# The order of copies, casts, sums and loads in one stage of a Fourier-mixing kernel

## The chip, the core and the metric

The kernel runs on one core of one Trainium2 chip. The metric is the device time of one execution in microseconds (us). TensorE is PE in the profile, its weight loads are PEld, VectorE is DVE, ScalarE is ACT, GpSimd is POOL, and SyncE (SP) issues most of the DMAs.

## What is computed

The input x has 2048 rows of 448 numbers. It is normalised, goes through a Fourier mixing and through a gated feed-forward network, and the two are multiplied:

```
xn = _layernorm(x, axis=-1)
# _A_ref
a = jnp.einsum("bsd,ed->bse", xn, dft_hid_re)
b = jnp.einsum("bsd,ed->bse", xn, dft_hid_im)
s = jnp.einsum("ts,bse->bte", dft_seq_re, a) - jnp.einsum("ts,bse->bte", dft_seq_im, b)
# _B_ref
g = _silu((_gelu(xn @ w_gate) * (xn @ w_up)) @ w_down)
return x + s * g
```

## The kernel before

The work has three parts, one behind the other: the feed-forward network (up to about 396 us of the span), the stage that computes a and b (396 to 484 us), and the sums along the sequence (from 484 us to the end). Numbers are kept in two parts, a high one that ACT casts from the full number and a low one that DVE gets as the difference, so a product takes two or three matmuls.

**The stage of a and b.** The 2048 rows are 16 tiles of 128. Tiles 0 to 7 are computed plainly: `hid_mm` issues 22 matmuls into two of the eight PSUM banks (a in one, b in the other). The other eight are computed as four pairs, tile 8+kk with tile 12+kk, by products of sums that save matmuls: `hid_pair` issues 39 matmuls into five banks, x1 (5 matmuls), x2 (6), x3 (5), x4 (5), then six more on top of x1, x6 (6), and six more on top of x4. Banks are given out in turn, so the one that was used eight tiles of PSUM ago must have been read.

After the matmuls a plain tile k goes through these steps: `hid_sums` has ACT copy the two banks into a scratch f in SBUF, `f_sums` has DVE make four differences within it (four instructions), `hid_split` has ACT cast the seven columns of f to the high part in the tile's place `TS[k]` (the 128x1568 ACTIVATE), and the function that it returns has DVE make the low part (the 128x1568 TENSOR_TENSOR). For tiles 0 to 3 the result is stored to DRAM (`td`), since its place is needed again. A pair has, between its products: ACT copies x1 to a scratch u (line 1298), DVE adds x2 to it (1301), makes c21 with x3 (1305) and a half of f with x4 (1288), ACT copies x1 again after its second round (1313), DVE makes another half with x6 (1288) and the last one with u and x4 (1321); then sums, casts and low parts for both tiles as above. The six matmuls on top of x1 can't start before ACT has copied x1 the first time; the six on top of x4 can't start before DVE has read x4 (the first use of line 1288).

Order of issue: tiles 0 and 1, pair 0, tile 2, pair 1, tile 3, pair 2, pair 3, then tiles 4 to 7. Within that, every engine does its instructions strictly in the order in which the program gives them. In the kernel before, the cast of tile 2 stands ahead of pair 1's first copy of x1 on ACT, and so for the other pairs. The low part of the plain tile (`between`) stands between the fourth sum and the second round of x1.

**Scratch.** Tiles 0 to 3, 8 to 11 and 4 use one f, in `raw`; tile 5 has one of its own (`f5`, tag g0); tiles 6, 7 and 12 to 15 share `f1` (tag d0), so tile 7's copies out of PSUM must wait for the low part of tile 6.

**Chunk 1.** Tiles 4 to 7 read chunk 1 of the transposed input. Its SBUF place holds, during the pairs, sums that the pairs use as weights (`tq`), so the chunk lies in DRAM (`sp`) and is loaded back in four parts by `load_1`, each after the last use of its place in pair 3: part 3 after the product x2, part 2 after x3, part 0 after x4, part 1 after x6. Each part is one DMA of 512 KB, for high and low together. `hid_mm(4, 1)` puts the matmuls on part 1 last and goes through parts 0, 2, 3 before.

**The sums along the sequence.** They go through units, one for each k and pair of output tiles. `load_c` loads a unit's two blocks on SP, `sum_c` has DVE make two sums, `prep_c` casts (ACT), makes the low part (DVE) and starts the next load into the freed place. `seven` issues a unit's 14 matmuls, in seven banks; the seventh product of unit 0 goes to the bank that held tile 7's a. In the kernel before, units 4, 5, 9 and 10 have their raw place in `cc`, units 0 to 3 and 6 to 8 in `raw`; from unit 11 on five places are used in turn. Unit 2's sums are made by POOL. Units 4 and 5 are loaded after tile 7's matmuls.

Of the kernel before, what the change touches and what calls it, by code (L numbers as in the profile page):

```python
# [48 lines left out]
LAST = 3  # L49

# [9 lines left out]
def fnet_geglu(ctx: ExitStack, tc: tile.TileContext, xw, ca, ct, cp, et, wss, wd, out):  # L60
# [495 lines left out]
    with tc.manual_schedule():  # L556
# [671 lines left out]
        def hid_mm(k, last=None):  # L1228
            c, kk = divmod(k, 4)
            sl = slice(kk * P, (kk + 1) * P)  # L1230
            ps = [in_turn("all", f"ab{k}_{r}") for r in range(2)]
            mm = [
                (r, (xtl if n == 2 else xth)[c][:, b, sl], e_at[b][r + 2 * (n == 1)], b == last)
                for r in range(2)
                for n in range(3)
                for b in range(3 if n == 1 else 4)
            ]
            mm = [v for v in mm if not v[3]] + [v for v in mm if v[3]]
            turn_ = [[i for i, v in enumerate(mm) if v[0] == r] for r in range(2)]
            for n, (r, a, b, _) in enumerate(mm):  # L1240
                nc.tensor.matmul(  # L1241
                    ps[r][:, :D], a, b, start=n == turn_[r][0], stop=n == turn_[r][-1],
                    skip_group_check=True,
                )
            return [p[:, :D] for p in ps]
# [9 lines left out]
        def hid_pair(kk, between, load):  # L1255
# [3 lines left out]
            fs[kc], fs[ke] = f_at(kc), f_at(ke)  # L1259
# [9 lines left out]
            t, q = ts[1], tq[1]  # L1269

            def run(ps, *jobs, first=True):
                mm = []
                for x_, e in jobs:
                    if isinstance(e, tuple):
                        mm += [(x_[i], e[j]) for i, j in ((0, 0), (0, 1), (1, 0))]
                    else:
                        mm += [(v, e) for v in x_]
                for n, (a, b) in enumerate(mm):
                    nc.tensor.matmul(  # L1279
                        ps, a[:, sl], b, start=first and n == 0, stop=n == len(mm) - 1,  # L1280
# [3 lines left out]
            def x_tile(i):  # L1284
                return in_turn("all", f"hx{i}_{kk}")[:, :D]

            def minus(to, a, ps):
                nc.vector.scalar_tensor_tensor(
                    to, two_sides(a), -1.0, two_sides(ps), op0=ALU.mult, op1=ALU.subtract
# [3 lines left out]
            fc, fe = fs[kc], fs[ke]  # L1293
            ea, eb = (two_sides(fe[:, :D]), two_sides(fe[:, D : 2 * D])) if plain_ else (halves(fe, 0), halves(fe, 1))
            u, c21 = temps
            x1 = x_tile(1)
            run(x1, (b11, a11), (k3, e_at[3][0]))
            nc.scalar.activation(u, x1, AF.Copy)
            x2 = x_tile(2)
            run(x2, (t[2], s2), (q[2], s2q))  # L1300
            nc.vector.tensor_add(u, u, x2)
            load(3)
            x3 = x_tile(3)
            run(x3, (t[3], s3), (q[3], s3q))
            nc.vector.tensor_add(c21, u, x3)
            load(2)
            x4 = x_tile(4)
            run(x4, (t[1], s1), (q[1], s1q))
            minus(eb, c21, x4)
            load(0)  # L1310
            between()
            run(x1, (b21, a12), (k2[0], k2a), first=False)
            nc.scalar.activation(halves(fc, 0), two_sides(x1), AF.Copy)
            x6 = x_tile(6)
            run(x6, (t[4], a22), (q[4], k2b))
            minus(halves(fc, 1), c21, x6)
            load(1)
            f_sums(kc)
            low_c = hid_split(kc)
            run(x4, (b22, s4), (k2[1], s4q), first=False)  # L1320
            nc.vector.tensor_add(ea, two_sides(u), two_sides(x4))
            if plain_:
                h, l = [rest(v) for v in ((new["tmp"], a_x[0]), (new["u1"], new["u0"]))[ke - 14]]
                nc.scalar.activation(h, fe[:, : 2 * D], AF.Copy)
                low_c()
                nc.vector.tensor_sub(l, fe[:, : 2 * D], h)
                ab[ke] = [(h[:, r * D : (r + 1) * D], l[:, r * D : (r + 1) * D]) for r in range(2)]
            else:
                f_sums(ke)
                low_e = hid_split(ke)  # L1330
                low_c()
                low_e()
# [46 lines left out]
        nxt = {0: 3, 1: 6, 2: 7, 3: 8, 9: None, 10: None}  # L1379
# [35 lines left out]

        def prep_c(m):

            if m >= len(units):
                return
            n = (4 if isinstance(units[m][1], str) else 7) * P  # L1420
            h, l = [v[:, :n] for v in slot_at(m)]
            split(h, l, raw_at(m)[:, :n])
            c_hl[m] = h, l
            n = nxt.get(m, m + 5)
            if n:
                load_c(n)


        def load_1(k):

            v, w = [u.rearrange("p (i k d) -> p i k d", i=2, k=4)[:, :, k] for u in (a_x[1].bitcast(F32), sp)]
            nc.sync.dma_start(v, w)
# [5 lines left out]
        ps = hid_mm(0)  # L1438
        late[0]()
        late[1]()  # L1440
        for _ in range(3):
            send()
        hid_sums(0, ps)()
        low_ = hid_split(0)
        for _ in range(3):
            send()
        low_()
        while dq:
            send()
        nc.sync.dma_start(gs[:, 8 * D :], gacc[2].tensor[:, : 8 * D])  # L1450
        hid_sums(1, hid_mm(1))()
        behind = hid_split(1)
        hid_pair(0, behind, lambda k: None)
        for k in (2, 3):
            hid_sums(k, hid_mm(k))()
            behind = hid_split(k)
            hid_pair(k - 1, behind, lambda k: None)
        hid_pair(3, lambda: None, load_1)
        load_c(0)
        load_t(0, a_x[0])  # L1460
        load_t(1, place("g1", 8 * D))
        hid_sums(4, hid_mm(4, 1))()
        behind = hid_split(4)
        ps = hid_mm(5)
        behind()
        load_c(1)
        load_c(2)
        hid_sums(5, ps)()
        behind = hid_split(5)
        sum_c(0)  # L1470
        prep_c(0)
        ps = hid_mm(6)
        behind()
        hid_sums(6, ps)()
        behind = hid_split(6)
        sum_c(1)
        sum_c(2, nc.gpsimd)
        behind()
        sum_c(3)
        ps = hid_mm(7)  # L1480
        cc = sb.tile([P, 4 * D], F32, name="cc", tag="d1")
        load_c(4)
        load_c(5)
        prep_c(1)
        sums7 = hid_sums(7, ps)
        prep_c(2)
# [95 lines left out]
        for m, (j, k) in enumerate(units):  # L1582
# [87 lines left out]
            else:  # L1670
                if m:
                    prep_c(m + 3)
                if m == 4:
                    sums7()
                if m == 6:
                    hid_split(7)()
                    load_c(14)
                    load_c(15)
# [72 lines left out]
```

## Time and profile before

| | |
|---|---|
| median of 3 runs | 779.63 us (777.25 to 779.84) |
| the profiled execution | 779.22 us, of which 777.4 us are the span of the trace |
| mean granted clock of TensorE | 0.996 |
| busy, share of the span | PE 98%, PEld 88%, DVE 84%, ACT 46%, POOL 16% |

The span is read from the first to the last instruction of the program; all times of the trace below are counted from its start. "Idle before" in a row, in square brackets, is the time for which the engine stood still just before it, and what ended that.

### The profile page before, as it was taken

Reading aid. Unit: us, or ns where it says so; the run is one execution under the profiler, and the core shown is the slowest. Engines: PE = TensorE matmul, PEld = TensorE weight load, DVE = VectorE, ACT = ScalarE, POOL = GpSimd, SP = SyncE. Lnnn points to the kernel's source line nnn. Section 1 sums busy time; section 2 is a strip of 40 time slices with the busy share of each in tenths; the row PEclk is TensorE's granted clock in tenths of the full one; section 3 lists DMA queues with packets and bytes.
Section 4 is the critical chain, followed back from the end, with each engine's and each line's share of the span. In section 5 each row is a group of like instructions: output and inputs, shape, how many; then the busy total and the mean of one; then the engine's idle time right before and its main releaser. Section 6 shows DMA issues by size and latency. Waiting matters only on the chain.

```text
span 777.4 us, 11575 instructions
## 1 busy us (share of the span) xinstructions
PE 761.6 (98%) x4033; PEld 685.3 (88%) x4033; DVE 655.9 (84%) x1119; ACT 354.6 (46%) x511; POOL 121.9 (16%) x162
## 2 busy tenths in 40 slices
PE   9999999999999999999999879899999999999997
PEld 8988888888888888888889769899999999999997
DVE  7987788989999889998876875979788797979796
ACT  6866443434444344353433434545444444544451
POOL 1001422324133232232200001000000000000000
PEclk9999999999999999999999999999999999999999
DMA  8077574949486867658715265779696969788794
GB/s 292 17 220 229 126 237 134 276 138 256 151 220 217 233 247 174 212 161 256 202 52 250 93 223 219 228 232 302 233 337 212 342 218 331 221 282 280 248 307 152
DMA packets 83579, 170.31 MB, mean 219 GB/s; under 512 B 8256, under 2 KB 63424, under 8 KB 81728
## 3 DMA queue, kind: packets, MB, share of 16 engines
q1 hardware_dynamic: 78192, 143.05, 53.3%
q0 software_dynamic: 5184, 26.41, 15.7%
q8 instruction: 31, 0.51, 0.3%
q14 instruction: 28, 0.23, 0.1%
q10 hardware_dynamic: 144, 0.11, 0.0%
HBM read 146.01 MB, written 52.63 MB: 256 GB/s over the span
## 4 chain that ended last, share of the span: by engine, by line
PE 78%; DVE 13%; DMA 4%; ACT 3%; issue 2%; SPq 0%; DVEq 0%; ACTq 0%
PE p L1520 19%; PE x L449 18%; PE po L423 14%; PE p L1523 9%; PE py L1546 4%; PE x L461 3%; PE gu L372 3%; PE ab L1241 2%; PE gu L605 2%; PE hx L1279 1%; DMA xt<-sp 1%; DMA raw<-sums 1%; PE pt L207 1%; PE warm L574 1%; DMA out<-cc 1%
## 5 line engine op out<-in xcount | busy, mean ns | idle before, releaser
L423 PE MATMUL po<-wd,hs 128*128 128x448 f32 x672 | 146.2, 366 | 0.0
L423 PEld LDWEIGHTS po<-wd,hs 128*128 128x128 f32 x672 | 125.7, 188 | 12.5 <-DVE gacc L436 0.3
L449 PE MATMUL x<-xt,w 128*128 128x512 f32 x432 | 112.2, 390 | 0.0
L449 PEld LDWEIGHTS x<-xt,w 128*128 128x128 f32 x432 | 80.9, 188 | 16.3 <-DVE tmp L503 0.4
L449 PE MATMUL x<-t,w 128*128 128x512 f32 x276 | 80.4, 391 | 0.4 <-DVE tmp L539 0.4
L150 ACT ACTIVATE w<-raw 128x896 fp32r<-128x896 f32 (+1 forms) x59 | 53.6, 910 | 55.6 <-PE p L1520 25.6
L436 DVE TENSOR_TENSOR gacc<-gacc,po 128x448 f32<-128x448 f32 x96 | 58.6, 614 | 5.5 <-PE po L423 5.2
L526 ACT ACTIVATE hs<-tmp 128x512 fp32r<-128x512 f32 x24 | 15.2, 633 | 104.1 <-DVE tmp L524 104.1
L449 PEld LDWEIGHTS x<-t,w 128*128 128x128 f32 x276 | 51.7, 188 | 10.7 <-DVE tmp L539 0.8
L1520 PE MATMUL p<-xt,xt 128*128 128x448 f32 x168 | 54.8, 376 | 2.4 <-ACT f L1346 2.4
L1520 PE MATMUL p<-ts_g,w 128*128 128x448 f32 x168 | 55.5, 380 | 0.0
L1572 POOL DMA_DIRECT2D cc<-xw x14 | 12.3, 881 | 257.5 <-DVE raw L1411 96.1
L321 POOL TENSOR_TENSOR raw<-raw 128x256 f32<-128x256 f32 x23 | 18.9, 823 | 214.5 <-DMA raw<-wss 143.4
L150 ACT ACTIVATE w<-f 128x896 fp32r<-128x896 f32 (+1 forms) x34 | 30.2, 888 | 38.1 <-PE p L1520 14.8
L151 DVE TENSOR_TENSOR w<-raw,w 128x896 fp32r<-128x896 f32 (+1 forms) x40 | 41.8, 1045 | 4.4 <-ACT w L150 4.1
L1523 PE MATMUL p<-ts_g,w 128*128 128x224 f32 x168 | 44.9, 267 | 0.0
L1523 PE MATMUL p<-xt,xt 128*128 128x224 f32 x168 | 44.6, 265 | 0.0
L1241 PE MATMUL ab<-w,xt 128*128 128x448 f32 x128 | 35.3, 379 | 2.5 <-DMA xt<-sp 2.5
L1520 PE MATMUL p<-xt,w 128*128 128x448 f32 x112 | 36.4, 374 | 0.0
L1520 PEld LDWEIGHTS p<-xt,xt 128*128 128x128 f32 x168 | 31.6, 188 | 5.1 <-ACT f L1346 2.7
L1520 PE MATMUL p<-hs,w 128*128 128x448 f32 x112 | 36.0, 374 | 0.0
L1520 PEld LDWEIGHTS p<-ts_g,w 128*128 128x128 f32 x168 | 32.2, 192 | 2.5
(302 smaller groups left out, 1860.8 us busy)
## 6 DMA issues: line engine op xcount, KB each, us to landing
sums<-ca SPq DMA_DIRECT2D x16, 896.0 KB, 8.6
sums<-ca POOLq DMA_DIRECT2D x16, 896.0 KB, 9.3
raw<-ct SPq DMA_DIRECT2D x69, 192.0 KB, 4.3
raw<-wss SPq DMA_DIRECT2D x24, 512.0 KB, 3.7
xt<-td SPq DMA_DIRECT2D x24, 448.0 KB, 5.5
ts_g<-td SPq DMA_DIRECT2D x24, 448.0 KB, 6.3
raw<-sums SPq DMA_DIRECT2D x69, 128.0 KB, 4.2
f<-ct SPq DMA_DIRECT2D x39, 192.0 KB, 4.7
```

The source lines that it names most:

```text
L150: nc.scalar.activation(h, src, AF.Copy)
L151: nc.vector.tensor_sub(l, src, h)
L321: eng.tensor_add(r[:, 1:16:14], r[:, 0:14:13], r[:, 9:17:7])
L372: nc.tensor.matmul(ps[:, cols], a, xt[:, k, cols], start=n == 0, stop=n == len(mm) - 1)
L423: nc.tensor.matmul(po[:, :D], hs[:, a, kk * P : (kk + 1) * P], wdn[:, b, i], start=n == 0, stop=n == 5,)
L436: nc.vector.tensor_add(ga, ga, po[:, :D])
L449: nc.tensor.matmul(ps, a[i], b[j], start=first and n == 0, stop=n == 2, skip_group_check=True)
L461: nc.tensor.matmul(ps, a[0], x_, start=False, stop=True, skip_group_check=True)
L1241: nc.tensor.matmul(ps[r][:, :D], a, b, start=n == turn_[r][0], stop=n == turn_[r][-1], skip_group_check=True,)
L1520: nc.tensor.matmul(ps[q][:, :D], h, v, start=u % UN == 0, stop=False, skip_group_check=True)
L1523: nc.tensor.matmul(ps[q][:, :HD], l, v[:, :HD], start=False, stop=u % UN == NS - 1, skip_group_check=True,)
L1546: nc.tensor.matmul(p[:, e], w, v[:, e], start=n == 0, stop=n == 11)
```

## The change

All of it lies in the stage of a and b and the first units; the arithmetic is the same, and no matmul is added or left out. The calls that were written out one by one (`hid_pair`, `hid_mm`, `load_1` and so on) become small steps with names, and a list, `HID`, gives their order. In that order:

1. In each pair ACT copies x1 for the first time ahead of the cast of the plain tile before it.
2. The tail of a pair is mixed with the next one's start. For pairs 2 and 3, ACT casts for tile 14 and tile 10 after pair 3's first copy of x1, and DVE makes the low part of tile 14 between pair 3's c21 and its read of x4, and that of tile 10 behind that read. Tile 0's low part stands behind the last sums of the feed-forward network.
3. Chunk 1 is loaded in eight DMAs of 256 KB, high and low apart, at the same four points. Tile 4's matmuls go through parts 3, 2, 0, 1, tile 7's through 2, 0, 1, 3.
4. Scratch: tiles 4 and 5 get a double one (`f45`, tag g0), tile 7 gets `cc`, and units 4, 5, 9 and 10 get the places in `f1` (tag d0), so that every unit but the first follows one rule of five places in turn.
5. Units 1 and 2 are loaded ahead of the large loads of k = 0 and 1 (`td`), unit 2's sums go from POOL to DVE, and the casts of units 0 to 2 come earlier: unit 1's and 2's wait for tile 7's matmuls on parts 2 and 0.

Two lines of the list, and the core of the rest:

```diff
+HID = """
...
+P1.x1 P1.m 2.ca P1.x2 P1.u P1.x3 P1.c21 P1.x4 P1.be 2.lo P1.x1b P1.ac P1.x6 P1.bc P1.sc P1.cc
...
+7.mm c.h1 c.d1 c.h2 c.d2 6.ca c.s3 6.lo c.l4 c.l5 7.ev
+"""
 
         def f_at(k):
-            if k == 5:
-                return sb.tile([P, 8 * HD], F32, name="f5", tag="g0")
-            if k in (6, 7, 12, 13, 14, 15):
+            if k in (4, 5):
+                if "f" not in new:
+                    new["f"] = sb.tile([P, 16 * HD], F32, name="f45", tag="g0")
+                return new["f"][:, 8 * HD * (k - 4) :][:, : 8 * HD]
+            if k == 7:
+                return cc
+            if k in (6, 12, 13, 14, 15):
...
+            if order:
+                mm.sort(key=lambda v: order.index(v[1]))
...
         def raw_at(m):
-            if m in (4, 5, 9, 10):
-                return cc[:, 896 * ((m + 1) % 5) :][:, :896]
-            i = (2, 0, 1, 2, 0, 0, 0, 1, 2)[m] if m < 9 else (m - 11) % 5
+            i = (m + 4) % 5 if m else 2
             return a_r[:, 896 * i :][:, :896] if i < 3 else new["d0"][:, 896 * (i - 3) :][:, :896]
...
         def load_1(k):
 
-            v, w = [u.rearrange("p (i k d) -> p i k d", i=2, k=4)[:, :, k] for u in (a_x[1].bitcast(F32), sp)]
-            nc.sync.dma_start(v, w)
+            for i in range(2):
+                v, w = [u[:, 2048 * i + 512 * k :][:, :512] for u in (a_x[1].bitcast(F32), sp)]
+                nc.sync.dma_start(v, w)
...
+        orders = {4: (3, 2, 0, 1), 7: (2, 0, 1, 3)}
...
+        for word in HID.split():
+            a, b = word.split(".")
+            if word == "7.ev":
+                cc = sb.tile([P, 4 * D], F32, name="cc", tag="d1")
+            steps_[a][b]()
```

In the list, `mm` is a plain tile's matmuls, `ev` its copies out of PSUM, `sm` its sums, `ca` its cast, `lo` its low part; of a pair, `x1` to `x6` are products (`x1b` and `x4b` the second rounds), `m` the first copy of x1, `u`, `c21`, `be`, `ac`, `bc`, `ae` the steps named above in that order, `sc`, `cc`, `lc` sums, cast and low part of the tile 8+kk and `se`, `ce`, `le` those of 12+kk; `x.0` to `x.3` are the loads of chunk 1, `t.0` and `t.1` the large loads, `c.l`, `c.s`, `c.h`, `c.d` a unit's load, sums, cast and low part.

On ACT, from tile 2 (`ab2`) to pair 1 (`hx1_1` is x1 of pair 1), before:

```order
L1346 ACTIVATE raw_76<-ab2_0_3604 128x2x224
L1347 ACTIVATE raw_76<-ab2_1_3605 128x2x224
L1358 ACTIVATE hs0_77<-raw_76 128x7x224
L1298 ACTIVATE raw_76<-hx1_1_3635 128x448
L1313 ACTIVATE raw_76<-hx1_1_3635 128x2x224
```

The same place on ACT in the changed kernel:

```order
L1374 ACTIVATE raw_76<-ab2_0_3600 128x2x224
L1375 ACTIVATE raw_76<-ab2_1_3601 128x2x224
L1341 ACTIVATE raw_76<-hx1_1_3634 128x448
L1386 ACTIVATE hs0_77<-raw_76 128x7x224
L1349 ACTIVATE raw_76<-hx1_1_3634 128x2x224
```

The first copy of x1 has moved ahead of the cast of tile 2 (into `hs0`), which itself waits for DVE's sums of tile 2.

On SP, from the loads of chunk 1 (`xt1` from `sp`) through the large loads (from `td0`, `td1`), before:

```order
L1432 DMA xt1_68<-sp_810 128x2x512 x4
L1404 DMA raw_76<-ct 128x384
L1405 DMA raw_76<-sums0_800 128x256
L1436 DMA xt0_67<-td0_3400 128x3136
L1436 DMA ts_g1_3858<-td1_3401 128x3136
```

The same place on SP in the changed kernel:

```order
L1459 DMA xt1_68<-sp_810 128x512 x8
L1427 DMA raw_76<-ct 128x384
L1428 DMA raw_76<-sums0_800 128x256
L1427 DMA raw_76<-ct 128x384
L1428 DMA raw_76<-sums0_800 128x256
L1427 DMA raw_76<-ct 128x384
L1428 DMA raw_76<-sums0_800 128x256
L1463 DMA xt0_67<-td0_3400 128x3136
L1463 DMA ts_g1_3890<-td1_3401 128x3136
```

Four loads have become eight, and the two large loads now stand behind the loads of units 0, 1 and 2 instead of unit 0 alone.

On DVE, from the low part of tile 6 (into `ts_g0`) to that of unit 4 (from `cc` into `xt3` and `xt2`), before:

```order
L1361 TENSOR_TENSOR ts_g0_3965<-f1_3537,ts_g0_3965 128x7x224
L1411 TENSOR_TENSOR raw_76<-raw_76 128x128
L1412 TENSOR_TENSOR raw_76<-raw_76 128x128
L151 TENSOR_TENSOR w_73<-raw_76,w_73 128x896 x2
L151 TENSOR_TENSOR xt1_68<-raw_76,w_73 128x896
L1411 TENSOR_TENSOR cc_3998<-cc_3998 128x128
L1412 TENSOR_TENSOR cc_3998<-cc_3998 128x128
L1411 TENSOR_TENSOR cc_3998<-cc_3998 128x128
L1412 TENSOR_TENSOR cc_3998<-cc_3998 128x128
L151 TENSOR_TENSOR xt3_70<-cc_3998,xt2_69 128x896
```

The same place on DVE in the changed kernel, where units 4 and 5 lie in `f1`:

```order
L1446 TENSOR_TENSOR w_73<-raw_76,w_73 128x896 x2
L1434 TENSOR_TENSOR raw_76<-raw_76 128x128
L1435 TENSOR_TENSOR raw_76<-raw_76 128x128
L1389 TENSOR_TENSOR ts_g0_4005<-f1_3535,ts_g0_4005 128x7x224
L1446 TENSOR_TENSOR xt1_68<-raw_76,w_73 128x896
L1434 TENSOR_TENSOR f1_3535<-f1_3535 128x128
L1435 TENSOR_TENSOR f1_3535<-f1_3535 128x128
L1434 TENSOR_TENSOR f1_3535<-f1_3535 128x128
L1435 TENSOR_TENSOR f1_3535<-f1_3535 128x128
L1446 TENSOR_TENSOR xt3_70<-f1_3535,xt2_69 128x896
```

The low parts of units 1 and 2 have moved ahead of tile 6's, and units 4 and 5 are summed in the place from which tile 6's low part is made just before.

More of the change, by code (lines that the diff above doesn't have):

```diff
@@ L1269, in hid_pair, with run @@
             t, q = ts[1], tq[1]
-            def run(ps, *jobs, first=True):
+            ps = {}
+            u, c21 = temps
+            def run(i, *jobs):
+                first = i not in ps
+                if first:
+                    ps[i] = in_turn("all", f"hx{i}_{kk}")[:, :D]
                 mm = []
@@ L1303, in hid_pair @@
[L1303 to L1322, printed above, removed]
+            def side(k, r):
+                if k in KP:
+                    return two_sides(fs[k][:, r * D : (r + 1) * D])
+                return halves(fs[k], r)
+            def begin():
+                fs[kc], fs[ke] = f_at(kc), f_at(ke)
+                run(1, (b11, a11), (k3, e_at[3][0]))
@@ L1436, in load_t @@
             nc.sync.dma_start(TS[k].bitcast(F32), td[k])
[L1438 to L1486, printed above, removed]
+        ps_of, sums_of = {}, {}
+        def tile_steps(k, order=None):
+            return {
+                "mm": lambda: ps_of.update({k: hid_mm(k, order)}),
+                "ev": lambda: sums_of.update({k: hid_sums(k, ps_of[k])}),
+                "sm": lambda: sums_of[k](),
+                "ca": lambda: low_of.update({k: hid_split(k)}),
+                "lo": lambda: low_of.pop(k)(),
+            }
```

127 lines of the change are left out of this document (77 added, 50 removed).

## The prediction

> **What bounds the kernel now.** First the page: TensorE is busy almost throughout, so only its gaps and slow stretches can be won.
>
> ```profile
> span 777.4 us, 11575 instructions
> PE 761.6 (98%) x4033; PEld 685.3 (88%) x4033; DVE 655.9 (84%) x1119; ACT 354.6 (46%) x511; POOL 121.9 (16%) x162
> ```
>
> Then the waits of PE over the whole run (columns: us in total, times, longest). All four below lie in the stage that is changed.
>
> ```profile
> PE hx L1279 <- ACT raw L1298: 4.3, 3, 1.9
> PE ab L1241 <- DMA xt<-sp: 2.5, 1, 2.5
> PE p L1520 <- ACT f L1346: 2.4, 1, 2.4
> PE hx L1279 <- DVE f L1288: 0.8, 1, 0.8
> ```
>
> Next PE's timeline: the starts of pair 0 and pair 1, the first of the three waits on line 1298, tiles 4 and 5, unit 0, the wait inside unit 0, units 2 and 5.
>
> ```profile
> 415.03 1.18 PE L1279 MATMUL hx<-w,xt 128*128 128x448 f32 x5
> ...
> 427.39 1.18 PE L1279 MATMUL hx<-w,xt 128*128 128x448 f32 x5
> ...
> 433.70 0.88 PE L1279 MATMUL hx<-wd,xt 128*128 128x448 f32 x3 [1.88 <-ACT raw L1298]
> ...
> 464.73 4.87 PE L1241 MATMUL ab<-w,xt 128*128 128x448 f32 x16 [2.54 <-DMA xt<-sp]
> ...
> 470.65 0.36 PE L1241 MATMUL ab<-w,xt 128*128 128x448 f32 x1
> ...
> 484.03 0.36 PE L1520 MATMUL p<-xt,xt 128*128 128x448 f32 x1
> ...
> 488.50 0.74 PE L1520 MATMUL p<-xt,xt 128*128 128x448 f32 x1 [2.44 <-ACT f L1346]
> ...
> 492.55 0.38 PE L1520 MATMUL p<-hs,w 128*128 128x448 f32 x1
> ...
> 499.13 0.38 PE L1520 MATMUL p<-ts_tmp,w 128*128 128x448 f32 x1
> ```
>
> From pair 0's start to pair 1's, with no wait, 39 + 22 = 61 matmuls take 12.36 us: 0.2026 us each. That is the pace of the stage. Units 2 to 4 give the units' pace: (499.13 - 492.55) / 3 = 2.19 us. Last the windows; the number ahead of the DMA share is the granted clock.
>
> ```profile
> 448.00:450.00 2.00, 1.62 (x8) 1.52 (x9) 1.44 (x3) 0.32 (x1) 0.00 (x0) 1.00 0.04 8
> ...
> 464.00:466.00 2.00, 1.27 (x3) 1.16 (x4) 1.86 (x2) 0.94 (x2) 0.00 (x0) 0.58 0.94 286
> 466.00:468.00 2.00, 2.00 (x7) 1.80 (x6) 0.93 (x1) 0.00 (x0) 0.00 (x0) 0.57 0.97 287
> ...
> 488.00:490.00 2.00, 1.50 (x5) 1.38 (x6) 1.61 (x4) 2.00 (x4) 0.00 (x0) 0.55 0.00 0
> 490.00:492.00 2.00, 2.00 (x10) 1.85 (x9) 2.00 (x3) 0.56 (x1) 0.00 (x0) 0.59 0.62 174
> ```
>
> Behind the waits of 2.54 and 2.44 us the clock is about half for some 3 us; behind one of the waits on line 1298, of at most 1.9 us (the first row), it stays whole. So two of the waits cost more than their length.
>
> **What all gaps together are worth.** (1) From pair 1's start to tile 4 there are 3 x 39 + 22 = 139 matmuls: 28.16 us at the pace, so tile 4 could start at 455.55 instead of 464.73. That is 9.18 us, of which 7.64 are the named waits up to there (4.3 + 0.8 + 2.54) and the rest is drained pipeline and slow matmuls just behind them. (2) Tile 4 takes 470.65 - 464.73 = 5.92 us for 22 matmuls that need 4.46: 1.46 us of half clock. (3) Units 0 and 1 take 492.55 - 484.03 = 8.52 us instead of 4.38: 4.14 us. The sum is 14.78 us; below I take away what stays.
>
> **The pairs.** Rows of DVE and ACT between tile 2 and pair 1, and the start of the same DVE steps one round later:
>
> ```profile
> 430.20 0.38 DVE L1336 TENSOR_TENSOR raw<-raw 128x224 f32<-128x224 f32 x1
> ...
> 431.22 0.39 DVE L1339 TENSOR_TENSOR raw<-raw 128x224 f32<-128x224 f32 x1
> ...
> 431.70 1.51 ACT L1358 ACTIVATE hs<-raw 128x1568 fp32r<-128x1568 f32 x1 [2.05 <-DVE raw L1339]
> ...
> 433.12 0.53 ACT L1298 ACTIVATE raw<-hx 128x448 f32<-128x448 f32 x1
> 433.68 0.62 DVE L1301 TENSOR_TENSOR raw<-raw,hx 128x448 f32<-128x448 f32 x1 [2.07 <-ACT raw L1298]
> ...
> 435.67 1.78 DVE L1361 TENSOR_TENSOR hs<-raw,hs 128x1568 fp32r<-128x1568 f32 x1
> ...
> 444.87 0.39 DVE L1336 TENSOR_TENSOR raw<-raw 128x224 f32<-128x224 f32 x1
> ```
>
> ACT stands idle for 2.05 us before the cast, which waits for DVE's sums; the copy of x1, whose 5 matmuls were done at about 428.6, queues behind that cast, and PE and DVE wait for it. Ahead of the cast the copy runs in ACT's idle time, at about 429. The cast isn't late by it: its sums end by 431.6, as before. So the wait goes. What is late next is DVE: a round of it takes 444.87 - 430.20 = 14.67 us, less the 2.07 of idle time 12.60, against 12.36 of PE. It loses 0.24 a round but starts a good 1 us ahead, since pair 0's copy goes ahead of its cast too. The second round on x4 must find the first read of x4 done: by these durations it is ready about 1 us early in pairs 1 and 2. For pair 3 the same copy, now ahead of two casts, leaves about as much, although tile 14's low part (about 1.1 us) stands in between on DVE. I take 0 for what is left of the waits; the bounds are 0 and 0.7 (three rounds of 0.24).
>
> **Chunk 1.** The store of tile 3 and the four loads, the store's issue first, then the issues of the loads (shortest, median and longest in ns, first and last start in us), then size and us to landing of tile 2's store, which ran alone, and of the first and the last load:
>
> ```profile
> 452.77 0.54 POOL L1363 DMA_DIRECT2D td<-xt  x1 [14.20 <-issue]
> ```
>
> ```profile
> L1432 SPq DMA_DIRECT2D xt<-sp x4: 519/818/1211, 454.6 to 459.9; - x4
> ```
>
> ```profile
> td<-hs POOLq DMA_DIRECT2D x1, 1568.0 KB, 5.3
> ```
>
> ```profile
> xt<-sp SPq DMA_DIRECT2D x1, 512.0 KB, 7.5
> ```
>
> ```profile
> xt<-sp SPq DMA_DIRECT2D x1, 512.0 KB, 6.1
> ```
>
> The first load landed at 462.1, 9.3 us after the store's issue, the last (issued at 459.9) at 466.0: 1.3 us from one part to the next. Now DVE's sums of tile 3 start 2.07 + 1.0 us earlier than 444.87, at 441.8, its low part ends 5.2 us later (435.67 + 1.78 - 430.20 - 2.07 in the round before), near 447.0, and the store goes out near 447.6; part 3 can be loaded from 449.9 (pair 3 at 447.65, 11 matmuls in), parts 2 and 0 from 450.9 and 451.9, part 1 from 454.3. If part 3 again lands 9.3 us behind the store, it is there at 456.9 and the others at 458.2, 459.5 and 460.8; if the store is out of the way after 5.3 us, at about 454. Tile 4 needs part 3 at 455.55, part 2 at 456.4, part 0 at 457.6, part 1 at 458.8 (4, 6 and 6 matmuls apart). So the wait that is left is 2.0 us at the one end, 0 at the other; the store now has 2.3 us head start instead of 1.8, so I take 1.2, spread over four short waits that leave the clock whole. The eight issues cost SP nothing that anyone waits for: behind them stands unit 0's load, needed 10 us later. The two large loads now stand behind units 1 and 2, out at about 462 and due at 474.
>
> The Trainium skill ("DMA: Bandwidth & Descriptors", "Anatomy of one DMA") counts a fixed 2.0 us per DMA and speaks for few large ones: paid one after another, by estimate from that page eight parts would take 8 x 2.6 us, four 4 x 3.2, the last would land near 470.7, and about 12 of the 14.78 us would be gone. The 1.3 us between parts above says that the fixed part overlaps.
>
> **Tile 7 and the units.** Rows of what DVE does here, and of the loads of unit 4 in the kernel before:
>
> ```profile
> 483.81 0.33 SPq L1404 DMA_DIRECT2D cc<-ct  x1
> ...
> 486.07 1.79 DVE L1361 TENSOR_TENSOR ts_g<-f,ts_g 128x1568 fp32r<-128x1568 f32 x1 [1.11 <-ACT ts_g L1358]
> 487.79 0.28 DVE L1411 TENSOR_TENSOR raw<-raw 128x128 f32<-128x128 f32 x1
> 488.10 0.29 DVE L1412 TENSOR_TENSOR raw<-raw 128x128 f32<-128x128 f32 x1
> 488.31 1.08 DVE L151 TENSOR_TENSOR w<-raw,w 128x896 fp32r<-128x896 f32 x1
> ```
>
> ```profile
> raw<-ct SPq DMA_DIRECT2D x1, 192.0 KB, 2.4
> ```
>
> With `cc` as scratch, tile 7's copies wait for PE and ACT alone, not for the low part of tile 6 (486.07 to 487.86), and unit 0's seventh product finds its bank free. In exchange units 4 and 5 are loaded into tile 6's scratch, behind that low part, where before they went out at 483.81 without it. Behind pair 3's last products (455.55) DVE has sums, one addition and two low parts (1.4, 0.6, 1.75, 1.1) and waits for two casts, which takes it to about 461.5. From there: three plain tiles at 1.4 + 1.75, units 0 to 2 at 0.6 + 1.05, unit 3's sums 0.6, together 15.0, so tile 6's low part ends near 476.5. Four issues of some 0.4 us and 2.4 us to landing bring unit 5 in by 481; its sums and unit 4's low part end near 482.6. PE wants that at 455.55 + 1.2 + 88 x 0.2026 + 4 x 2.19 = 483.3. I take 0.1; the ends are 0 and 3.0 (below). Unit 2's sums cost DVE 0.6 us, counted here.
>
> **Sum.** 14.78 - 0 - 1.2 - 0.1 = 13.5 us off the profiled 779.22 gives 765.7. That execution lies 0.4 us under the median of 779.63, within the runs' spread. Behind the units PE stays the bound, so the gain is kept to the end.
>
> **The rivals.**
>
> *Tile 4 waits as long as before.* If the loads stay 7.5 us behind their issue while the new order makes tile 4 begin with the first of them, PE waits some 2.5 us in one piece and the half clock stays: 14.78 - 2.54 - 1.46 = 10.8, so 768.4. For it: 1568 KB of store and 2 MB of load still overlap. Against: tile 4 now starts with the part that is issued first, not the third. By the Trainium skill ("TensorE: Matmul & The Clock Gate", "Part 1") the clock halves only after an idle window of about 3.4 us, by which the 1.46 us would not be lost and this rival would give 767.0. The rows above show half clock behind 2.54 us, so I keep it.
>
> *Unit 4 is late.* If its loads take 6.1 us instead of 2.4, as the last part of chunk 1 did among others, DVE ends unit 4's low part 3.7 us later, at 486.3: 3.0 us of wait for PE and, as behind the 2.44, some 1.5 of half clock, so 14.78 - 1.2 - 3.0 - 1.5 = 9.1: 770.1. For it: one strict queue on DVE. Against: nothing large is left to load by then.
>
> *The pairs' waits only move.* DVE at 12.60 against 12.36 can make the second round on x4 wait where that on x1 did. If it gives back all of 4.3 + 0.8 and the pipeline's share, some 5.8 us, the time is 771.5. Against it: DVE's 2.07 us of idle time in each round, which this frees.
>
> *Slower: the eight loads go one after the other.* If each part waits for the one before and takes its own time to landing, say 4.2 us (halfway between 2.4 for 192 KB alone and 6.1 for 512 KB among others), the last lands at 449.9 + 8 x 4.2 = 483.5 and tile 4 ends 1.2 us later, at 484.7 instead of 470.65: 14.0 lost and 4.1 won in units 0 and 1, so 789.1. The kernel becomes slower by over 3.9 us from 3.45 us a part upward ((470.65 + 4.14 + 3.9 - 1.2 - 449.9) / 8). Against it: the parts landed 1.3 us apart, each 6 to 8 us behind its issue, so several were under way at once.
>
> **How the numbers follow.** Forecast 0.68 (764 to 767.5), tile 4 0.14, unit 4 0.08, the pairs 0.06, one after the other 0.02, nothing that I name 0.02. The range 763.5 to 771 leaves out the last two and what lies past 771 of the others. About 0.5%, 3.9 us, is what a measurement of this kernel can tell from no change: all but the last two and a mixture of two rivals are faster by more, 0.94; within, 0.04; slower, 0.02.
>
> **What would show it.** Right: no wait on line 1341 in pairs 1 to 3, tile 4's start at 455 to 457, tile 7's copies right behind its matmuls, unit 5's start near 486, clock 1.0 throughout. Wrong: a wait of over 2 us anywhere before unit 5, or DVE's read of x4 behind PE.

## The result and the profile after

The changed kernel takes 767.20 us (median of 4 runs, 766.22 to 767.89) against 779.74 (4 runs, 777.25 to 781.42): ratio 0.984, 95% interval 0.981 to 0.987. The forecast was 765.7, its range 763.5 to 771.0. The profiled execution took 767.89 us, the longest of the four; its span is 766.1 against 777.4.

The page's first rows, then the waits of PE over the whole run (us in total, times, longest):

```profile
span 766.1 us, 11581 instructions
PE 757.9 (99%) x4033; PEld 681.8 (89%) x4033; DVE 658.0 (86%) x1121; ACT 355.0 (46%) x511; POOL 119.7 (16%) x160
```

```profile
PE ab L1266 <- DMA xt<-sp: 1.5, 1, 1.5
PE warm L590 <- PEq L1743: 0.8, 1, 0.8
```

Of the four waits that the prediction listed, only that for the loads of chunk 1 is left, at 1.5 us instead of 2.5. The second row is the kernel's start and was there before. PE's timeline at the places that were shown of before: pair 0, pair 1, the second round on x1 in it, tile 4 with its wait, tile 5, units 0, 2 and 5.

```profile
415.86 1.18 PE L1305 MATMUL hx<-w,xt 128*128 128x448 f32 x5
...
428.23 1.18 PE L1305 MATMUL hx<-w,xt 128*128 128x448 f32 x5
...
432.48 0.77 PE L1305 MATMUL hx<-wd,xt 128*128 128x448 f32 x3
...
456.40 2.37 PE L1266 MATMUL ab<-w,xt 128*128 128x448 f32 x10
460.30 1.70 PE L1266 MATMUL ab<-w,xt 128*128 128x448 f32 x6 [1.54 <-DMA xt<-sp]
...
463.09 0.37 PE L1266 MATMUL ab<-w,xt 128*128 128x448 f32 x1
...
476.73 0.37 PE L1524 MATMUL p<-xt,xt 128*128 128x448 f32 x1
...
481.11 0.38 PE L1524 MATMUL p<-hs,w 128*128 128x448 f32 x1
...
487.92 0.37 PE L1524 MATMUL p<-ts_tmp,w 128*128 128x448 f32 x1
```

Pair 0 starts 0.83 us later than before, by small waits in the feed-forward network that the change doesn't touch. So the stage is best read from pair 0's start on. To unit 5 it takes 487.92 - 415.86 = 72.06 us, before 499.13 - 415.03 = 84.10: 12.04 us less, where the prediction's sum said 13.5. From unit 5 to the end both need the same within 0.2 us. 12.04 less the 0.83 is the span's 11.3, within 0.1. The medians differ by 12.5, since the profiled execution before lay 0.5 us under its median and the one after 0.7 above.

Why the pairs run through is seen on ACT and DVE beside pair 1 (tile 2's second copy, the first copy of x1, tile 2's cast; then DVE's last sum of tile 2, the addition of x2, the first read of x4, tile 2's low part, and the start of tile 3's sums):

```profile
428.96 0.54 ACT L1375 ACTIVATE raw<-ab 128x448 f32<-128x448 f32 x1
429.44 0.55 ACT L1341 ACTIVATE raw<-hx 128x448 f32<-128x448 f32 x1
431.55 1.52 ACT L1386 ACTIVATE hs<-raw 128x1568 fp32r<-128x1568 f32 x1 [1.56 <-DVE raw L1367]
```

```profile
430.04 0.38 DVE L1364 TENSOR_TENSOR raw<-raw 128x224 f32<-128x224 f32 x1
...
431.06 0.39 DVE L1367 TENSOR_TENSOR raw<-raw 128x224 f32<-128x224 f32 x1
431.37 0.61 DVE L1343 TENSOR_TENSOR raw<-raw,hx 128x448 f32<-128x448 f32 x1
...
432.81 0.62 DVE L1311 SCALAR_TENSOR_TENSOR f<-raw,hx 128x448 f32<-128x448 f32 x1
433.35 1.78 DVE L1389 TENSOR_TENSOR hs<-raw,hs 128x1568 fp32r<-128x1568 f32 x1
...
442.54 0.38 DVE L1364 TENSOR_TENSOR raw<-raw 128x224 f32<-128x224 f32 x1
```

The copy now runs in ACT's idle time, the cast still starts right behind DVE's sums, and DVE goes on without a gap. A round of DVE takes 442.54 - 430.04 = 12.50 us instead of 14.67. Its first read of x4 ends at 433.4, and PE comes to the second round on x4 at 434.9.

### The profile page after: what moved, and what is told of

Its sections match the earlier page's. It is cut to its first block, busy times and chain, and to the rows that moved or that the text cites. A ratio compares the mean times of both kernels' runs of the same rounds, so it can differ in the third digit from the quotient of the medians.

```text
span 766.1 us, 11581 instructions
## 1 busy us (share of the span) xinstructions
PE 757.9 (99%) x4033; PEld 681.8 (89%) x4033; DVE 658.0 (86%) x1121; ACT 355.0 (46%) x511; POOL 119.7 (16%) x160
## 4 chain that ended last, share of the span: by engine, by line
PE 86%; DVE 8%; DMA 2%; issue 2%; ACT 1%; SPq 0%; DVEq 0%
PE p L1524 21%; PE x L465 19%; PE po L439 15%; PE p L1527 10%; PE ab L1266 4%; PE py L1550 4%; PE hx L1305 4%; PE x L477 3%; PE gu L388 3%; PE gu L621 2%; PE pt L223 1%; DMA xt<-sp 1%; DVE tmp L562 1%; DVE ew L1054 1%; DVE gacc L452 1%
## 5 line engine op out<-in xcount | busy, mean ns | idle before, releaser
L439 PEld LDWEIGHTS po<-wd,hs 128*128 128x128 f32 x672 | 125.7, 188 | 12.5 <-DVE gacc L452 0.3
L1442 ACT ACTIVATE w<-f 128x896 fp32r<-128x896 f32 (+1 forms) x37 | 33.0, 892 | 40.5 <-PE p L1527 15.5
L356 ACT ACTIVATE w<-raw 128x768 fp32r<-128x768 f32 x24 | 20.2, 843 | 31.8 <-POOL raw L343 31.6
```

The costliest lines, as they stand in the source:

```text
L439: nc.tensor.matmul(po[:, :D], hs[:, a, kk * P : (kk + 1) * P], wdn[:, b, i], start=n == 0, stop=n == 5,)
L1442: nc.scalar.activation(c_hl[m][0], raw_at(m)[:, :n], AF.Copy)
```

## The experiments

Each kernel is the changed one with one edit, unless it says otherwise. All were timed against the kernel before, which took 778.1 to 779.5 us (medians) beside them. The ratios are to it; the changed kernel's is 0.984. "Behind pair 0" means behind the first matmul of pair 0 in the same trace; unit 0 is there at 60.9 us and unit 5 at 72.1 in the changed kernel.

**1. The casts ahead of the copies again** (in all four pairs).

```diff
-P1.x1 P1.m 2.ca P1.x2 P1.u P1.x3 P1.c21 P1.x4 P1.be 2.lo P1.x1b P1.ac P1.x6 P1.bc P1.sc P1.cc
+P1.x1 2.ca P1.m P1.x2 P1.u P1.x3 P1.c21 P1.x4 P1.be 2.lo P1.x1b P1.ac P1.x6 P1.bc P1.sc P1.cc
...
-P3.x1 P3.m P2.ce P2.cc P3.x2 x.3 P3.u P3.x3 x.2 P3.c21 P2.le P3.x4 x.0 P3.be P2.lc P3.x1b P3.ac
+P3.x1 P2.ce P2.cc P3.m P3.x2 x.3 P3.u P3.x3 x.2 P3.c21 P2.le P3.x4 x.0 P3.be P2.lc P3.x1b P3.ac
```

> The changed kernel, but in every pair ACT's cast stands ahead of its first copy of x1 again, as before the change. Theory (the copies behind the casts cost PE the waits on line 1298 and, through DVE, the one on 1288): 4.3 + 0.8 us of wait come back, 5.8 with the drained pipeline, so 772.3 to 773.0 against 767.2; the waits stand at the second round on x1, about 1.9 us each at most, and the clock stays whole. Rival (DVE's 12.6 us a round bounds the pairs in either order): the waits only change their line, and the time is within 1 us of 767.2.

774.1 us (773.4 to 777.5, 10 runs), ratio 0.995 (0.994 to 0.997). PE's waits:

```profile
PE hx L1305 <- ACT raw L1341: 5.0, 3, 2.0
PE p L1527 <- DVE xt L1446: 1.6, 1, 1.6
...
PE p L1524 <- ACT xt L1442: 0.7, 1, 0.7
PE hx L1305 <- DVE f L1311: 0.4, 1, 0.4
```

The rival falls: the waits of before come back at the second round on x1, with the rest of the change untouched. Tile 4 starts 47.05 us behind pair 0 instead of 40.54, 6.5 later. The loads of chunk 1 then are in time, which gives 2.2 back. But the expectation missed the second and third rows: DVE's queue is late for the whole rest of the stage, and PE waits for it again in unit 4. By unit 6 the loss is 9.65 us in this execution, part of it half clock in units 4 and 5; at 776.3 us it is one of the four slower ones of the ten, so the medians' 6.9 us is the fairer size.

**2. Chunk 1 in four loads.**

```diff
-            for i in range(2):
-                v, w = [u[:, 2048 * i + 512 * k :][:, :512] for u in (a_x[1].bitcast(F32), sp)]
-                nc.sync.dma_start(v, w)
+            v, w = [u.rearrange("p (i k d) -> p i k d", i=2, k=4)[:, :, k] for u in (a_x[1].bitcast(F32), sp)]
+            nc.sync.dma_start(v, w)
```

> The changed kernel, but chunk 1 comes in four loads of 512 KB as before, at the same points and for the same order of tile 4. Theory (from 453.5 to 461.5 us the DMA engines are 77 to 102% busy, so the bytes set when a part lands, not the number of DMAs): PE starts each part of tile 4 when its later half would have come, so 0 to 0.6 us longer, 767.2 to 767.8, wait at tile 4 of 1.5 to 2.2 us. Rival 1 (each DMA costs a fixed time, SP's issues of 1.15 and 1.24 us among it): the parts land earlier, the wait of 1.5 us goes, 765.7. Rival 2 (eight parts are what made tile 4 early): the wait at tile 4 grows above 2.5 us in one piece with half clock behind it, 770 or more.

766.7 us (766.1 to 767.2, 4 runs), ratio 0.985 (0.983 to 0.987): no difference from the changed kernel that can be measured. The wait at tile 4 is now two short ones:

```profile
455.83 1.07 PE L1266 MATMUL ab<-w,xt 128*128 128x448 f32 x4 [0.41 <-DMA xt<-sp]
457.31 2.85 PE L1266 MATMUL ab<-w,xt 128*128 128x448 f32 x12 [0.40 <-DMA xt<-sp]
```

Rival 2 falls: the eight parts gain nothing. SP's part in it shows in the issues, for the changed kernel and this one (shortest, median and longest in ns, first and last start):

```profile
L1459 SPq DMA_DIRECT2D xt<-sp x8: 320/379/1237, 450.7 to 456.0; - x8
```

```profile
L1458 SPq DMA_DIRECT2D xt<-sp x4: 518/585/775, 449.8 to 454.2; - x4
```

In the changed kernel two of the eight issues take 1.15 and 1.24 us, and part 0 goes out 38.7 us behind pair 0; with four it goes out at 37.1. Tile 5 starts at 46.5; with the eight loads it starts at 46.7 to 47.2 in three traces (the changed kernel's, experiments 4 and 5). So rival 1 is half right: with the store under way, eight issues instead of four cost part 0 some 1.6 us on SP, of which 0.2 to 0.7 reaches PE.

**3. Tile 4 in the old order of parts.**

```diff
-        orders = {4: (3, 2, 0, 1), 7: (2, 0, 1, 3)}
+        orders = {4: (0, 2, 3, 1), 7: (2, 0, 1, 3)}
```

> The changed kernel, but tile 4 goes through the parts of chunk 1 in the order 0, 2, 3, 1, close to that of the kernel before. Part 0 landed at 460.3 (high) and 460.9 us (low), tile 4 could start at 456.4, so PE waits about 3.9 us in one piece. Theory (behind a wait of over some 2.4 us the clock is half for about 3 us, as in the kernel before): tile 4 ends at 460.3 + 4.5 + 0.6 + 1.46 = 466.8 instead of 463.1, so +3.7: 770.9. Rival (the half clock of the kernel before had another reason): whole clock, tile 4 ends at 465.3, +2.2: 769.4.

770.2 us (768.7 to 770.8, 5 runs), ratio 0.989 (0.987 to 0.991). PE's row for tile 4, and the granted clock (ahead of the DMA share) in stretches of 3.41 us around it:

```profile
457.90 5.33 PE L1266 MATMUL ab<-w,xt 128*128 128x448 f32 x16 [2.24 <-DMA xt<-sp]
```

```profile
454.68:458.09 3.41, 1.17 (x6) 0.76 (x5) 3.01 (x7) 1.25 (x2) 0.00 (x0) 1.00 1.01 342
458.09:461.50 3.41, 3.33 (x9) 2.45 (x9) 2.57 (x2) 1.65 (x2) 0.00 (x0) 0.50 0.56 196
```

By the medians the order of the parts is worth 3.0 us. The trace shows one wait of 2.24 instead of 1.54 and half clock behind it, by which tile 5 starts 2.1 us later behind pair 0 and unit 5 1.6 us later. This execution, at 768.8 us, is one of the two quicker ones of five; what the others (770.2 to 770.8) lose beyond that was not seen. The wait was shorter than expected, since PE got part 0 1.5 us earlier behind pair 0 than in the trace of the changed kernel, with the same loads.

**4. The old scratch**: tile 7 in `f1`, the units' places and their next loads as before.

```diff
-            if k == 7:
-                return cc
-            if k in (6, 12, 13, 14, 15):
+            if k in (6, 7, 12, 13, 14, 15):
...
+            if m in (4, 5, 9, 10):
+                return cc[:, 896 * ((m + 1) % 5) :][:, :896]
...
```

> The changed kernel, but tile 7 uses tile 6's scratch again, and the units have the places of the kernel before (units 4 and 5 in cc). The order of the list stays. Theory 1 (scratch alone gave the 4.1 us of units 0 and 1, as the prediction's third step reads): a wait of about 2.4 us on tile 7's first copy in unit 0 and half clock behind it, 771.3. Theory 2 (the low part of tile 6 ends at 479.2 us, the first copy at 479.6, unit 0 starts at 476.7 and comes to its seventh product at 478.6): a wait of 1.0 us, whole clock, 768.2. Rival (hidden anyway): within 0.3 us of 767.2.

768.6 us (768.1 to 770.2, 4 runs), ratio 0.988 (0.986 to 0.990).

```profile
477.52 0.47 PE L1526 MATMUL p<-xt,xt 128*128 128x448 f32 x1 [1.72 <-ACT f L1372]
```

Theory 2's mechanism, with a longer wait: 1.72 us and whole clock, and 1.4 us in the time. Units 0 and 1 take 6.35 us here, 8.52 in the kernel before and 4.38 in the changed one. So the scratch alone is not the 4.1 us of the prediction's third step but about half of it. The other half goes with what this kernel keeps, the list's order above all: with the order alone (experiment 6) the two units take 5.74 us.

**5. That wait made longer**: experiment 4, and tile 7's first copy three times.

```diff
+            for _ in range(3 if k == 7 else 1):
+                nc.scalar.activation(f[:, 0:8:7], ps[0].rearrange("p (i d) -> p i d", i=2), AF.Copy)
```

> The kernel with the old scratch, but tile 7's first copy out of PSUM is made three times, which makes PE's wait in unit 0 longer by two copies of 0.43 us: 1.72 + 0.86 = 2.58 us instead of 1.72. Theory (the clock goes to half behind a wait of some 2.2 to 2.5 us, as at tile 4 with the old order, and stays whole behind 2.0): half clock for about 3 us, 768.6 + 0.86 + 1.5 to 1.9 = 771.0 to 771.4. Rival (the clock halves only behind an idle window of about 3.4 us, as the Trainium skill has it in TensorE: Matmul & The Clock Gate, Part 1): whole clock, 769.5.

770.9 us (768.3 to 773.7, 6 runs), ratio 0.991 (0.989 to 0.993).

```profile
479.29 0.47 PE L1527 MATMUL p<-xt,xt 128*128 128x448 f32 x1 [2.28 <-ACT f L1373]
```

```profile
477.35:480.76 3.41, 1.47 (x9) 1.42 (x10) 0.31 (x2) 2.91 (x5) 0.00 (x0) 1.00 0.79 230
480.76:484.17 3.41, 3.41 (x14) 3.14 (x13) 2.80 (x6) 1.79 (x2) 0.00 (x0) 0.50 0.31 97
484.17:487.58 3.41, 3.41 (x24) 3.25 (x24) 2.96 (x7) 0.95 (x1) 0.00 (x0) 1.00 0.56 145
```

A wait of 2.28 us brings half clock for 3.41 us; one of 1.72 at the same place did not. In two of the six runs (768.3 and 769.3 us) the mean clock is 0.999, in the others 0.994 to 0.997: the clock is not halved there every time. How long the wait was in the runs without a trace isn't known.

**6. Of the change only the list's order**: the edits of experiments 2, 3 and 4 together.

> Of the change only the list's order stays: four loads, tile 4's order 0, 2, 3, 1 and the scratch of the kernel before. Theory 1 (the parts add up as single reversals measured them: four loads -0.5, tile 4's order +3.0, scratch +1.4): 771.1. Theory 2 (not additive: PE's longer stop at tile 4 gives DVE the time to finish tile 6's low part, so that the wait on tile 7's copies goes): 769.7 to 770.2, with a wait of 3.4 us at tile 4 and none in unit 0. Rival (the order alone does everything): within 1 of 767.2.

771.1 us (768.3 to 771.6, 6 runs), ratio 0.991 (0.989 to 0.993) as the three single reversals add up. Theory 2 falls: PE waits 3.37 us at tile 4 and still 1.10 for tile 7's copy. That is less than the 1.72 of experiment 4, so its mechanism is there in part.

**7. The store of tile 3 behind the large loads**, on SP. By then t.0 has overwritten tile 3's place, so this kernel stores other data, and its sums with tile 3 are others; what runs and when is as meant.

```diff
-                if k in td:
+                if k in td and k != 3:
...
-4.mm P3.ce P3.lc P3.le c.l1 c.l2 t.0 t.1 4.ev 4.sm 4.ca c.s0 c.s1
+4.mm P3.ce P3.lc P3.le c.l1 c.l2 t.0 t.1 3.st 4.ev 4.sm 4.ca c.s0 c.s1
...
+                "st": lambda: nc.sync.dma_start(td[k], TS[k].bitcast(F32)),
```

> The changed kernel, but tile 3's store is issued on SP behind the large loads (t.1) instead of on POOL ahead of chunk 1's loads. Theory (store and loads share DMA engines that are 77 to 102% busy, so the store's 1568 KB are what makes tile 4 wait): alone, each part lands some 2.4 to 3 us behind its issue, ahead of PE; the wait of 1.5 us at tile 4 goes, tile 5 starts 45.0 instead of 47.2 us behind pair 0, and the time is about 765.0 against 767.2. Rival 1 (the loads' own time or SP's slow issues bound it): the wait stays, 767.2. Rival 2 (the store now holds up unit 3's load, or the large loads, and PE waits there): 767 to 770, with a wait in units 0 to 5.

772.2 us (770.2 to 773.4, 6 runs), ratio 0.993 (0.991 to 0.994). Tile 4 and the first matmul of tile 5:

```profile
455.48 3.40 PE L1266 MATMUL ab<-w,xt 128*128 128x448 f32 x16
458.72 1.38 PE L1266 MATMUL ab<-wd,xt 128*128 128x448 f32 x6
459.94 0.36 PE L1266 MATMUL ab<-w,xt 128*128 128x448 f32 x1
```

The theory's mechanism and rival 2 both hold, rival 2 at a higher price than its 767 to 770. Tile 4 runs 22 matmuls in 4.46 us without a wait, so the store is what made it wait. But the store now waits for t.0 on SP and goes out at 471.1. Unit 3's load, right behind it, takes 8.4 us to landing (5.4 in the changed kernel), DVE stands 5.84 us for it, and the loads of units 4 and 5 go out only after that: PE waits four times, 1.25 to 1.65 us, in units 3 and 4. With four loads as well:

> Both: tile 3's store behind the large loads, and chunk 1 in four loads of 512 KB. Theory (bytes on the DMA engines decide, the number of loads does not): as with the store moved and eight loads, 765.0, within 0.5. Rival (with the store out of the way the fixed share of a DMA counts, and four are better): 764.0 or less. Rival 2 (now the size of a part decides, since PE waits for the first whole part): a wait at tile 4 of about 0.5 us, 765.5 or more.

772.8 us (772.4 to 774.2, 6 runs), ratio 0.994 (0.992 to 0.995): the same loss in the units; tile 5 starts at 45.4 us behind pair 0, as rival 2 had it.

**8. The store right behind the last load of chunk 1**, on SP; the store's own lines are those of experiment 7.

```diff
-P3.x6 x.1 P3.bc P3.sc P3.cc P3.x4b P3.ae c.l0
+P3.x6 x.1 3.st P3.bc P3.sc P3.cc P3.x4b P3.ae c.l0
```

> The changed kernel, but tile 3's store is issued on SP right behind the last load of chunk 1 (x.1), ahead of the large loads, instead of on POOL ahead of chunk 1. Theory (the store is what made tile 4 wait, as with the store behind the large loads, where tile 4's matmuls ran without a wait; and here nothing of units 1 to 4 stands behind it for long): tile 5 starts 45.0 us behind pair 0 instead of 47.2, unit 5 69.9 instead of 72.1, 765.0 us against 767.2. Rival (DVE's queue is late for unit 4 already in the changed kernel, by 0.24 us, and does not move with PE): the gain turns into a wait in unit 4, 766.7 to 767.2. Rival 2 (unit 0's load and the large loads now come late behind the store): a wait in units 0 to 2, over 767.2.

768.9 us (767.1 to 771.4, 6 runs), ratio 0.987 (0.984 to 0.989). Tile 5 starts at 45.8 instead of 47.2, but unit 5 at 74.4 instead of 72.1. DVE's rows tell why: unit 3's first sum, tile 6's low part behind it, and the first sum of unit 4, whose load may go out only then.

```profile
478.53 0.29 DVE L1434 TENSOR_TENSOR raw<-raw 128x128 f32<-128x128 f32 x1 [1.77 <-DMA raw<-sums]
...
479.07 1.78 DVE L1389 TENSOR_TENSOR ts_g<-f,ts_g 128x1568 fp32r<-128x1568 f32 x1
...
483.74 0.29 DVE L1434 TENSOR_TENSOR f<-f 128x128 f32<-128x128 f32 x1 [1.89 <-DMA f<-sums]
```

Neither rival as written: the gain goes in unit 4, but by way of unit 3's load. Behind the store the large loads go out 1.1 us later; unit 3's load, issued at the same distance from pair 0 (within 0.2 us), then takes 7.2 us to landing instead of 5.4, and DVE stood for it with tile 6's low part queued behind. This trace is of the slowest of the six runs (771.4). This is the prediction's rival "unit 4 is late", met in another kernel. With four loads too:

> The same with chunk 1 in four loads of 512 KB. Theory (bytes, not the number of loads): the first whole part lands some 0.4 us behind the need, as with four loads and the store behind the large loads (tile 5 at 45.4 us), so 765.0 to 765.5. Rival (SP's fewer issues bring the store and unit 0's load out earlier): below 764.7. Rival 2 (unit 4's wait on DVE takes the gain): 766.5 to 767.

768.8 us (768.2 to 771.3, 6 runs), ratio 0.987 (0.985 to 0.989); tile 4 waits 0.58 and 0.71 us for whole parts, and unit 5 starts at 71.9 us behind pair 0, hardly earlier than in the changed kernel. Why the time is then 1.6 us longer is seen only in part. In the trace (768.2) PE's last matmul still starts 0.15 us earlier behind pair 0 than in the changed kernel's; what is lost lies at the very end, where ACT stands 1.31 us for a load (`ts_g` from `gs`) ahead of three of its last copies. The traces of the changed kernel and of experiment 1 have no such wait; all others have it, the kernel before too, with 0.4 to 1.7 us. So a difference of 1 us or so between two of these kernels needn't come from the stage that was changed.

**9. The same with unit 3's sums behind tile 6's low part.**

```diff
-7.mm c.h1 c.d1 c.h2 c.d2 6.ca c.s3 6.lo c.l4 c.l5 7.ev
+7.mm c.h1 c.d1 c.h2 c.d2 6.ca 6.lo c.l4 c.l5 c.s3 7.ev
```

> As with the store behind x.1 and eight loads, but unit 3's sums stand behind tile 6's low part and the loads of units 4 and 5 on DVE, not ahead of them. Theory (there DVE stood 1.77 us for unit 3's load, which queued behind the large loads, and with it tile 6's low part, the loads of units 4 and 5 and at last PE in unit 4): tile 6's low part runs at 476.8, the loads of units 4 and 5 go out 2.2 us earlier, the wait in unit 4 shrinks to about 0.8 us, unit 5 starts about 71 us behind pair 0 (changed kernel 72.1, store behind x.1 alone 74.4), the clock stays whole, 766.1 against 768.9. Rival (unit 3 itself now becomes late: its load lands at 478.4, its low part is made at 480.3, PE wants it at 481.7): none of it unless the load lands a further 1.4 us later; then a wait ahead of unit 3 and 767 to 768. Rival 2 (the second store's traffic holds up the loads of units 4 and 5 as well): 768.9 as before.

766.4 us (765.3 to 768.5, 5 runs), ratio 0.985 (0.982 to 0.987). PE's two waits in the stage:

```profile
458.92 1.74 PE L1266 MATMUL ab<-wd,xt 128*128 128x448 f32 x6 [0.64 <-DMA xt<-sp]
483.69 0.37 PE L1528 MATMUL p<-w,xt 128*128 128x224 f32 x1 [0.65 <-DVE xt L1446]
```

The theory holds: the wait in unit 4 shrinks to 0.65 us, and unit 5 starts at 71.4. Against the changed kernel it is 0.8 us less by the medians, no more than the intervals allow.

## Why the prediction was right, point by point

- **The pairs: right.** No wait is left on the copy or on DVE's read of x4, and tile 4's first matmul comes 40.54 us behind pair 0; the forecast was 455.55 - 415.03 = 40.52. The rival of the moved waits had DVE's round at 12.60; it takes 12.50, and the read of x4 is 1.5 us early in pair 1, not 1.
- **Tile 4: the mis-sized term.** The 1.2 us are 2.23 in the trace (463.09 - 456.40 - 4.46), and "spread over four short waits" was wrong: parts 3 and 2 came in time, then PE stood 1.54 us for part 0 in one piece. In two other traces with the same loads (experiments 4 and 5) tile 4 loses 1.7 and 2.0. The sum put the landings between the store's 5.3 and 9.3 us and took a value in the middle; without the store the term is 0 (experiment 7), with it part 0 lands at the late end. A step of its own that failed is "The eight issues cost SP nothing that anyone waits for". Part 0's place was free at 452.7 (the forecast 451.9 and pair 0's 0.83), but SP was busy with two slow issues and sent it out at 454.52. Four loads instead of eight save PE 0.2 to 0.7 us of it. With the store out of the way the longest issue takes 0.39 us instead of 1.24 (experiment 8; 0.63 in experiment 7):

```profile
L1459 SPq DMA_DIRECT2D xt<-sp x8: 319/344/390, 450.8 to 455.7; - x8
```

- **The half clock: right in the sum.** The clock is whole from pair 0 to unit 5, and a wait of 2.24 us at the same place (experiment 3) brings half clock. So the 1.46 us belonged in the sum. The rule of the Trainium skill that the prediction cited, an idle window of about 3.4 us ("TensorE: Matmul & The Clock Gate", "Part 1"), would have left the clock whole behind 2.24 and 2.28 us; experiments 3 and 5 decide against it as the prediction read it.
- **Tile 7 and units 0 and 1: right in size, only partly for the reason given.** Unit 0 to unit 2 takes 4.38 us, the pace, and tile 7's copy starts at 477.1, right behind its matmuls. The prediction gave that to `cc` as scratch; experiment 4 shows 1.4 us in the time and 2.0 in these units for the scratch, with the rest going with the list's order.
- **Unit 4: 0.24 us instead of 0.1, in part by luck.** The rival had the price right in kind: as soon as the loads ahead of units 3 to 5 are pushed back (experiments 7 and 8), PE waits there. DVE's queue was later than worked out: by the rows below tile 6's low part ends at 479.17 and unit 4's at 485.77, which is 478.3 and 484.9 less pair 0's 0.83, where the prediction had 476.5 and 482.6. PE came to unit 4 at 485.50, in the same way 484.7, 1.4 us later than the 483.3 of the prediction, mostly by what tile 4 lost, and that hid most of it. Where PE comes there earlier (experiments 2, 8 and 9) it waits for the unit's cast or low part, 0.25 to 1.28 us at a time.

```profile
477.39 1.78 DVE L1389 TENSOR_TENSOR ts_g<-f,ts_g 128x1568 fp32r<-128x1568 f32 x1
...
484.69 1.08 DVE L1446 TENSOR_TENSOR xt<-f,xt 128x896 fp32r<-128x896 f32 x1
```

- **Not in the sum**: tiles 5 to 7 take 13.64 us in this execution (and in experiment 6) instead of 13.37, the value in experiments 1 to 3. The trace names no wait for it; it stays open. With tile 4 (1.03), unit 4 (0.14) and this (0.27) the 13.5 become the measured 12.0.
- **One load after the other: refuted.** Behind the store the eight loads land 0.5 to 0.8 us apart, except ahead of part 0 (2.6), and four loads or eight make no measurable difference, though one DMA takes 5.5 us (median) to landing with eight and 6.2 with four. A fixed time per DMA, paid in turn, isn't seen. The 2.0 us that the prediction took from the Trainium skill ("DMA: Bandwidth & Descriptors", "Anatomy of one DMA") stand there as a fit for DMAs issued from GpSimd, while these are issued on SP.

How the 12.5 us divide, by single reversals: the copies ahead of the casts 6.9, tile 4's order of parts 3.0, the scratch 1.4, the eight loads nothing that can be measured. Experiment 6 shows that the last three add up; for the copies it is assumed. What they leave, some 1.2 us, is then the rest of the list (tails mixed, units' loads and sums earlier), which was not reversed by itself.

## What to carry to other kernels

When an instruction that frees a buffer for the bound engine stands in a strict queue behind one that waits for a third engine, move it ahead: it cost nothing here and gave about half of the gain, and more than its waits, since the lateness went on to later units. Read a row of loads with the transfer that runs beside them and with what their issues cost on the queue. Moving a transfer out of one wait (experiments 7 and 8) moved the wait to the next load behind it, so follow each queue up to its next consumer before moving anything.

## What the runs showed of the hardware

In the rows below the granted clock goes by stretches of 3.41 us, each wholly at 1.00 or at 0.50. In the kernel before, the two halved stretches start at 464.31 and 488.20, which is 7 x 3.41 apart, so they lie on one grid; the Trainium skill ("TensorE: Matmul & The Clock Gate", "Part 1") says that the window runs freely, and this agrees. What the halved stretches go with is how busy PE was in the stretch before, more than the length of one wait (first number after the comma: PE's busy time). Rows of the kernel before, of experiment 4, of experiment 1 in the pairs and in the units, and of experiment 7 with four loads:

```profile
460.90:464.31 3.41, 1.29 (x6) 0.85 (x5) 2.28 (x7) 1.72 (x2) 0.00 (x0) 1.00 1.01 379
464.31:467.72 3.41, 2.99 (x8) 2.69 (x9) 2.62 (x2) 0.63 (x1) 0.00 (x0) 0.50 0.97 289
...
488.20:491.61 3.41, 3.11 (x11) 2.86 (x12) 3.06 (x4) 2.36 (x4) 0.00 (x0) 0.50 0.31 92
```

```profile
474.79:478.20 3.41, 1.69 (x11) 1.36 (x10) 2.00 (x3) 1.28 (x3) 0.00 (x0) 1.00 0.79 235
478.20:481.61 3.41, 3.41 (x24) 3.26 (x23) 2.23 (x6) 1.67 (x3) 0.00 (x0) 1.00 0.40 127
```

```profile
446.36:449.77 3.41, 1.79 (x9) 1.68 (x10) 1.60 (x3) 1.57 (x2) 0.00 (x0) 1.00 0.02 5
...
487.31:490.72 3.41, 1.80 (x10) 1.20 (x9) 1.56 (x5) 1.18 (x2) 0.00 (x0) 1.00 0.60 186
490.73:494.14 3.41, 2.76 (x10) 2.58 (x11) 3.34 (x7) 2.25 (x3) 0.00 (x0) 0.50 0.39 109
```

```profile
480.45:483.86 3.41, 1.65 (x9) 1.32 (x10) 2.18 (x2) 0.46 (x1) 0.00 (x0) 1.00 0.32 94
483.86:487.27 3.41, 2.64 (x9) 1.67 (x7) 1.22 (x5) 0.95 (x1) 0.00 (x0) 0.50 0.65 195
487.27:490.68 3.41, 2.41 (x8) 2.28 (x9) 3.34 (x7) 2.15 (x3) 0.00 (x0) 0.50 0.36 100
```

Behind stretches at whole clock with up to 1.47 us busy the next was halved; behind 1.69 and 1.79 it was whole, but behind 1.65 and 1.80 in the units it was halved, so the border lies near half of the stretch and isn't sharp in these modelled times. Behind a stretch that was halved itself it took more: with 2.41, 2.64 and 2.76 us busy the next was halved again, with 2.99 and 3.11 it was whole. A wait of 2.04 us that fell over two stretches cost no clock (the row at 446.36 holds 1.6 us of it). Two waits of 0.69 and 1.58 us close together did. A halved stretch costs up to 1.7 us, half of its length. Whether a wait of some 2 us brings one seems to depend on where it falls, which would be one reason why runs of one kernel differ; no run tests that by itself.
